# An attention and feed-forward kernel: its first loads, its idle products and its opening steps in another order

## The chip, the cores and the metric

The kernel runs on one core of one Trainium2 chip. The metric is the device time of one execution in microseconds (us); where several executions are shown, their median. Shorter is better.

The engines are named as in the profile: PE multiplies matrices, DVE (VectorE) and ACT (ScalarE) work on elements, POOL (GpSimd) does a little scalar work here, SP (SyncE) issues most of the transfers (DMAs). ACT issues a few of them at the start and at the end.

## The reference

Two parts follow each other. The first is an attention without softmax for 4 batches of 4 heads, 1088 positions and 32 columns each. A position's features are the 64 products of two sketches of 8 numbers, taken with the small matrices S1 and S2:

```python
def phi(x):
    a = np.einsum('rd,bhsd->bhsr', S1, x)
    b = np.einsum('rd,bhsd->bhsr', S2, x)
    return np.einsum('bhsi,bhsj->bhsij', a, b).reshape(*x.shape[:-1], r * r)
q_p, k_p = (phi(q), phi(k))
kv = np.einsum('bhsf,bhsd->bhfd', k_p, v)
z = np.sum(k_p, axis=2)
num = np.einsum('bhsf,bhfd->bhsd', q_p, kv)
den = np.einsum('bhsf,bhf->bhs', q_p, z)[..., None] + 1e-06
attn_out = num / den
```

The second part takes the 4352 resulting tokens of 128 columns through two matrix products with a rational function between them:

```python
h = x @ w_in                       # 128 -> 2048
P = a[0] + a[1] * h + a[2] * h**2 + a[3] * h**3
Q = 1.0 + np.abs(b[0]) * np.abs(h) + np.abs(b[1]) * h**2
out = (P / (Q + 1e-06)) @ w_out    # 2048 -> 128
```

## The kernel before

The whole program is one list of steps in an order written out by hand, `ORDER`, in the class `Fast`. (The class `General` is a second way through for coefficients that the first can't treat; it isn't entered here.) Each step is a name and a number, such as `kf1:0`. A loop goes through the list and emits each step's instructions on the engine that the step belongs to. Every engine then works through its own instructions strictly in that order; between engines only data and buffers are waited for. So a step's place in the list matters only against the other steps of the same engine. That holds for SP too, where the steps are transfers.

The opening, up to the first hidden layer, consists of these steps (the number behind the colon is a batch, a query block or a half):

- `load_v`, the two loads of S (into `s_raw`), those of the first batch's keys `k0`, of the first queries `q0`, and of `a` and `b` stand ahead of the list. The keys come in three transfers: the first four columns of each of four strips, the rest of three strips, and the rest of the last.
- `lx`, `lw`, `lk`, `lq`, `lv` load halves of `w_in`, halves of `w_out`, and keys, queries and v (`lq:0` is the rest of the first batch's queries). All are issued by SP.
- `tn` lets PE multiply a tile of zeros into a result that nobody reads, as often as `TURNS` says (`turn`, line 222).
- DVE turns S and spreads it (lines 250 and 255). Behind that, `kt0` to `kt3` turn the keys (line 315), `ks0` to `ks2` multiply them by S on PE (line 323), `kc` copies one sketch on ACT (line 330), `kf` multiplies the two sketches on DVE (line 335), and `kp0` to `kp2` multiply the features by v on PE (line 364). `kk` copies the sums (line 374).
- Query blocks go the same way: `qt` turns (DVE, line 387), `qs` sketches (PE, line 400), `qc` copies (ACT, lines 407 and 410), `qf` features (DVE, line 416), `qp` products with the keys' sums (PE, line 428), `qd`, `qi` and `qx` divide (lines 437, 444 and 449), `qb` turns back (PE, line 455), `qk` copies into `xT` (ACT, line 462). The blocks 0, 1 and 2 are the first three of the first batch; block 3 and all later ones send their sketches through memory and back (`Spread.copies`), on SP.
- `ba` takes the absolute values of b on ACT and starts a chain of small POOL instructions (`fitting`); `bi` is a reciprocal on DVE and more POOL work behind it (`factors`, line 775); `wo` scales halves of `w_out` by its results, on ACT or DVE (lines 711 and 713).
- `h2:0` is the first hidden layer (line 519), `e` its copy from PE's result buffer (line 525).

Behind the opening, a unit of tokens runs through the hidden layer, the rational function on DVE and ACT, and the second product (`G`, line 677), while the next batch's attention is interleaved. All of this is in `ORDER` too.

Of the kernel before, what the change touches and what calls it, by code (L numbers as in the profile page):

```python
# [28 lines left out]
pd0:0 u0:0 kc0:1 kc1:1 kf0:1 m0:0 kt0:2 ln1:0 h0:1 e2:1 kt1:2 ex1:0 e0:1 v0:0 rd1:0 h1:1 ks1:2 qs:4 kf1:1 h3:1 qt:5  # L29
e1:1 h1:2 v1:0 u0:1 qf:3 qc:4 ln0:0 kc1:2 e3:1 ex0:0 kp1:1 qp:3 pd1:1 kf1:2 h3:2 ln0:1 s1:0 e1:2 rd0:0 qd:3 qi:3 G3:0  # L30
h0:2 ex0:1 e3:2 kk:1 e0:2 G0:0 x1:0 G5:0 qx:3 u1:1 qf:4 qs:5 qp:4 s0:0 u0:2 ln1:1 h2:2 lq:2 lk:3 qc:5 qd:4 qi:4 ex1:1
qt:7 qx:4 qb:3 qk:3 qb:4 lv:2 qk:4 x0:0 rd0:1 m1:1 ks0:2 qs:7 e2:2 u1:2 ln0:2 rd1:1 h2:3 v0:1 h0:3 e2:3 h1:3 v1:1
kc0:2 kf0:2 kt1:3 s1:1 ex0:2 qt:9 qf:5 e0:3 e1:3 kt0:3 ln1:2 G3:1 G2:0 h3:3 x1:1 h0:4 qc:7 e3:3 h3:4 ra0:2 st:0 qp:5
ex1:2 qd:5 qi:5 e0:4 ra1:2 kp1:2 s0:2 qx:5 G0:2 qs:6 u1:3 pd1:2 e3:4 qb:5 h1:4 qk:5 m0:2 G0:1 m1:2 h0:5 s1:2 qf:7
ln0:3 qc:6 e1:4 ln1:3 h2:4 x0:2 v1:2 G2:1 e0:5 ex1:3 qt:8 x1:2 pd1:3 h3:5 G1:2 kk:2 e2:4 ks0:3 ex0:3 qp:7 u1:4 e3:5
qs:8 ln0:4 rd0:3 rd1:3 h2:5 qd:7 e2:5 G3:2 qf:6 qc:8 s1:3 h1:5 G2:2 kc0:3 ln1:4 G5:1 kf0:3 qi:7 e1:5 lq:3 ex0:4 ex1:4
h1:6 G5:2 m1:3 h3:6 qx:7 u1:5 G3:3 ra0:4 qs:9 qp:6 x1:3 G0:3 rd1:4 G2:3 e1:6 ln0:5 st:2 pd1:4 lv:3 s1:4 h0:6 e3:6
ln1:5 qd:6 qi:6 qb:7 qf:8 G4:3 qx:6 qk:7 h2:6 m1:4 e0:6 qc:9 G0:4 ex1:5 qb:6 qk:6 qp:8 qt:10 ks1:3 h2:7 e2:6 G3:4
ex0:5 u1:6 x1:4 e2:7 h0:7 qd:8 ln1:6 G5:3 rd1:5 qi:8 h3:7 G1:4 G5:4 qt:12 G1:3 e0:7 G2:4 pd1:5 rd0:5 ex1:6 e3:7 h1:7
m1:5 kc1:3 ra1:6 qf:9 ln0:6 qx:8 e1:7 qp:9 qs:10 ex0:6 v0:5 qd:9 h1:8 s1:5 G4:4 u1:7 pd1:6 qc:10 h3:8 e1:8 st:4 qt:11  # L40
v1:5 rd0:6 qi:9 qb:8 G3:5 ln0:7 kf1:3 e3:8 ln1:7 h0:8 h2:8 x1:5 qk:8 qs:11 e0:8 ex1:7 kp1:3 s1:6 qx:9 G0:5 e2:8 G5:5
ex0:7 h2:9 kk:3 qf:10 h3:9 u1:8 qb:9 ra0:7 m0:6 G0:6 ra1:7 qs:12 m1:6 qc:11 x0:6 ln0:8 v1:6 e3:9 pd1:7 e2:9 qp:10 qk:9
# [28 lines left out]
class General:  # L71
    FAST = False
    TURNS = (11, 0, 0, 0, 2, 0, 0, 0, 0)
# [49 lines left out]
def run(  # L123
# [70 lines left out]
    for i, s_in in enumerate((S1, S2)):  # L194
        t = consts.tile([128, D], FP, name=f"s_raw{i}")
        (nc.scalar, nc.sync)[i].dma_start(out=t, in_=bass.AP(tensor=s_in.tensor, offset=s_in.offset,
                                                             ap=[[0, 16], [D, R], [1, D]]))
        s_raw.append(t)
# [7 lines left out]
    nc.sync.dma_start(out=q0[:, 0:512], in_=q0_src[:, 0:512])  # L206
# [6 lines left out]
    nc.scalar.preload_act_table_set("abs_reciprocal_sqrt_and_small" if fast else "natural_log_exp_and_others")  # L213
    load_v(0)
# [59 lines left out]
    b_fit, c_fit, c_inv = (consts.tile([128, 2], FP, name=x) for x in ("b_fit", "c_fit", "c_inv"))  # L274
    a_k = consts.tile([128, 3], FP, name="a_k")
    special = consts.tile([128, 1], mybir.dt.int32, name="special")
    k_in_reg, k_sq_reg = (nc.scalar.alloc_register(x) if fast else None for x in ("k_in_reg", "k_sq_reg"))
    a1, a2, a3 = a_sb[:, 1:2], a_sb[:, 2:3], a_sb[:, 3:4]
# [370 lines left out]
    @skip()  # L649
    def d_v(i, h, hh):  # L650
        if horner(i, h):
            g = part_of(i, "g", h)
            nc.vector.tensor_scalar(out=g, in0=g, scalar1=a1, scalar2=None, op0=AX.add)

    @skip(plan.WIDE_X, horner)
    def d_g(i, h, hh):
        g = part_of(i, "g", h)
        nc.vector.tensor_mul(out=g, in0=g, in1=part_of(i, "s" if horner(i, first(h)) else "p", h))  # L658

    def terms(i):  # L660

        per = units[i][3]
        cuts = [(0, per // 2), (per // 2, per)]
        if i in plan.QUARTER:
            cuts[1:] = [(per // 2, 3 * per // 4), (3 * per // 4, per)]
        return [[(x, y, key) for x in range(*c)] if y != 1 or not horner(i, n) else []
                for n, c in enumerate(cuts) for y, key in enumerate(("r", "s", "g"))]
# [89 lines left out]
    def fitting():  # L757
        g = nc.gpsimd
        g.tensor_mul(out=sq, in0=ab0, in1=ab0)
# [5 lines left out]
        by(fit, b4, AX.is_ge, sq, AX.mult, fit)  # L765
        by(lim, fit, AX.mult, -1.0, AX.add, 1.0)
# [3 lines left out]
        g.tensor_copy(out=special, in_=lim)  # L770
        by(c_fit[:, 1:2], b4, AX.mult, 1.0 + 1e-6, AX.subtract, sq)
        g.tensor_copy(out=c_fit[:, 0:1], in_=b_fit[:, 0:1])

    def factors():
# [3 lines left out]
        nc.gpsimd.tensor_copy(out=a_k[:, 2:3], in_=k_out)  # L778
        by(k_in, b4, AX.mult, 0.5, AX.mult, c_inv[:, 0:1])
        by(k_sq, sq, AX.mult, c_inv[:, 1:2])  # L780

    def registers():
        nc.scalar.reg_load(k_in_reg, k_in[0:1, :].bitcast(mybir.dt.int32))
        nc.scalar.reg_load(k_sq_reg, k_sq[0:1, :].bitcast(mybir.dt.int32))
        if any(plan.P_ON_ACT):
            nc.scalar.reg_load(a3_reg, a_sb[0:1, 3:4].bitcast(mybir.dt.int32))
# [9 lines left out]
    does = {"e": evac, "h": hidden, "u": d_abs, "w": d_w, "y": d_y, "ln": a_square if fast else a_ln, "ex": a_root if fast else a_exp, "ra": a_inv, "rd": d_inv, "pa": a_p, "pd": d_p,  # L796
# [7 lines left out]
    for step in plan.ORDER:  # L804
# [63 lines left out]
```

## Time and profile before

| | |
|---|---|
| median of 3 runs | 251.57 us (251.22 to 251.88) |
| the profiled execution | 251.9 us |
| its span, first to last instruction | 250.0 us |
| PE busy | 240.5 us (96%) |
| DVE busy | 233.0 us (93%) |
| ACT busy | 227.9 us (91%) |
| POOL busy | 7.5 us (3%) |
| bytes moved | 19.60 MB, mean 78 GB/s |

Three engines are busy for over nine tenths of the span, so the busy time alone doesn't say which of them sets it. The profile's lines give a time from the span's start, a duration, the engine, the line of the code, the operation with its output and inputs, and in brackets how long the engine stood idle before it and what ended that. A number behind an x counts instructions; a matrix product in 32-bit floats appears as two of them.

### The profile page before, as it was taken

How to read it: one execution, taken by the hardware profiler on the slowest of the kernel's cores; microseconds unless marked ns; L12 is line 12 of the kernel's file. 1: busy time of each engine (PE TensorE's matmuls, PEld its weight loads, DVE VectorE, ACT ScalarE, POOL GpSimd, SP SyncE). 2: the span in 40 equal slices, each digit the busy share in tenths (PEclk: the TensorE clock that was granted, in tenths of full speed). 3: DMA queues.
4: the chain of work that ended last, by engine and by line, in shares of the span. 5: the costliest groups of instructions: out<-in, count | busy, mean ns of one | idle time of the engine just before them, and what ended most of it. 6: DMA issues, size and time to landing. Idle time of an engine off the chain costs nothing.

```text
span 250.0 us, 4083 instructions
## 1 busy us (share of the span) xinstructions
PE 240.5 (96%) x1585; PEld 133.8 (54%) x1585; DVE 233.0 (93%) x233; ACT 227.9 (91%) x217; POOL 7.5 (3%) x43
## 2 busy tenths in 40 slices
PE   7889999999999999999999999999999999999990
PEld 2668546645645455445555344444544467666770
DVE  3776999899999999999999999999999999999990
ACT  2267999999999999999999999999999999999980
POOL 4340000000000000000000000000000000000000
PEclk9999999999999999999999999999999999999999
DMA  5995348464413176210512200030020211020032
GB/s 155 257 387 89 99 121 188 134 156 78 144 27 100 28 202 138 69 45 16 148 22 77 67 3 0 16 102 3 0 42 0 40 25 22 0 37 8 0 49 42
DMA packets 30534, 19.60 MB, mean 78 GB/s; under 512 B 20400, under 2 KB 26672, under 8 KB 30512
## 3 DMA queue, kind: packets, MB, share of 16 engines
q1 hardware_dynamic: 28864, 18.92, 30.4%
q10 hardware_dynamic: 1648, 0.40, 0.9%
q8 instruction: 13, 0.21, 0.4%
q14 instruction: 9, 0.07, 0.1%
HBM read 16.16 MB, written 3.15 MB: 77 GB/s over the span
## 4 chain that ended last, share of the span: by engine, by line
PE 77%; DVE 13%; DMA 3%; issue 3%; SPq 0%; DVEq 0%
PE h_ps L519 42%; PE att_ps L677 23%; PE att_ps L428 4%; DVE g L658 4%; PE att_ps L364 4%; DVE g L647 3%; DVE s L643 2%; DMA k_sb<-in_k_dram 2%; PE att_ps L455 2%; DMA v_sb<-in_v_dram 2%; PE att_ps L473 2%; PE att_ps L323 1%; DVE p L600 1%; DVE r L630 1%; DVE out_sb L686 1%
## 5 line engine op out<-in xcount | busy, mean ns | idle before, releaser
L519 PE MATMUL h_ps<-xT,w_in_sb 128*128 128x512 f32 (+1 forms) x320 | 125.8, 532 | 0.0
L519 PEld LDWEIGHTS h_ps<-xT,w_in_sb 128*128 128x128 f32 x320 | 59.3, 190 | 44.4 <-issue 34.0
L525 ACT CAST hh<-h_ps 128x1024 bf16<-128x1024 f32 x68 | 72.2, 1086 | 2.1 <-PE h_ps L519 1.9
L613 ACT ACTIVATE ln<-u 128x2048 f32<-128x2048 bf16 (+1 forms) x35 | 67.2, 1950 | 0.0
L677 PEld LDWEIGHTS <-w_out 128*128 128x128 bf16 x432 | 41.8, 98 | 46.0 <-issue 16.5
L618 ACT ACTIVATE r<-ln 128x2048 bf16<-128x2048 f32 x22 | 44.0, 2002 | 0.0
L643 DVE TENSOR_TENSOR s<-hh,r 128x4096 bf16<-128x4096 bf16 (+2 forms) x21 | 39.2, 1872 | 0.0
L677 PE MATMUL att_ps<-r,w_out 128*128 128x512 bf16 (+1 forms) x160 | 34.8, 347 | 0.1
L677 PE MATMUL att_ps<-g,w_out 128*128 128x512 bf16 (+1 forms) x160 | 34.4, 347 | 0.0
L647 DVE TENSOR_TENSOR g<-hh,s 128x4096 bf16<-128x4096 bf16 (+2 forms) x16 | 27.8, 1744 | 0.3 <-PE att_ps L677 0.3
L658 DVE TENSOR_TENSOR g<-g,p 128x4096 bf16<-128x4096 bf16 (+2 forms) x15 | 27.7, 1849 | 0.0
L630 DVE TENSOR_TENSOR r<-r 128x2048 bf16<-128x2048 bf16 x22 | 26.5, 1217 | 0.0
L677 PE MATMUL att_ps<-s,w_out 128*128 128x512 bf16 (+1 forms) x112 | 24.5, 349 | 0.4 <-DVE s L643 0.4
L618 ACT ACTIVATE ln<-ln 128x2048 f32<-128x2048 f32 (+1 forms) x13 | 24.4, 1895 | 0.0
L624 ACT ACTIVATE r<-ln 128x2048 bf16<-128x2048 f32 (+1 forms) x13 | 23.7, 1868 | 0.0
L600 DVE TENSOR_SCALAR p<-hh,a_sb 128x4096 bf16<-128x4096 bf16 (+1 forms) x17 | 21.6, 1273 | 0.6 <-ACT hh L525 0.6
L548 DVE TENSOR_SCALAR u<-hh 128x2048 uint16<-128x2048 uint16 (+2 forms) x24 | 21.7, 905 | 0.4 <-ACT hh L525 0.4
L647 DVE TENSOR_TENSOR g<-hh,p 128x2048 bf16<-128x2048 bf16 (+1 forms) x7 | 11.6, 1663 | 0.0
L658 DVE TENSOR_TENSOR g<-g,s 128x2048 bf16<-128x2048 bf16 (+1 forms) x8 | 11.6, 1463 | 0.0
L428 PEld LDWEIGHTS att_ps<-kvz,q_pT 128*64 128x64 f32 x288 | 9.8, 137 | 3.3 <-issue 1.7
L428 PE MATMUL att_ps<-kvz,q_pT 128*64 128x66 f32 x288 | 11.1, 224 | 0.0
L364 PE MATMUL att_ps<-v_sb,k_p 128*64 128x64 f32 (+1 forms) x288 | 9.2, 222 | 1.0 <-DMA v_sb<-in_v_dram 1.0
(79 smaller groups left out, 146.6 us busy)
## 6 DMA issues: line engine op xcount, KB each, us to landing
a_all<-sk_d SPq DMA_DIRECT2D x6, 384.0 KB
b_all<-sk_d SPq DMA_DIRECT2D x12, 192.0 KB
v_sb<-in_v_dram SPq DMA_DIRECT2D x12, 144.0 KB
k_sb<-in_k_dram SPq DMA_DIRECT2D x3, 544.0 KB
q_sb<-in_q_dram SPq DMA_DIRECT2D x3, 544.0 KB
a_all<-sk_d SPq DMA_DIRECT2D x4, 320.0 KB
b_all<-sk_d SPq DMA_DIRECT2D x8, 160.0 KB
w_out_sb_f<-in_moe_w_out_dram SPq DMA_DIRECT2D x2, 512.0 KB
```

Of the source, the lines that this page charges most:

```text
L428: nc.tensor.matmul(self.nd[g * 64:(g + 1) * 64, o:o + 2 * KW], lhsT=self.q_p[:, c, x + g * 64:x + (g + 1) * 64], rhs=kvz[self.b % 2][:, c, ...
L519: nc.tensor.matmul(t[:, x * tl:(x + 1) * tl], lhsT=w_in_sb[:, f * 128:(f + 1) * 128], rhs=xT[:, x_at(t0):x_at(t0) + tl], start=True, stop= ...
L525: nc.scalar.copy(out=live[i]["hh"][:, part * PW:(part + 1) * PW], in_=live[i]["h", part])
L600: nc.vector.tensor_scalar(out=part_of(i, "p", h), in0=hh, scalar1=a3, scalar2=a2, op0=AX.mult, op1=AX.add)
L613: nc.scalar.activation(out=t, in_=live[i]["u"][:, span(h)], func=ACT.Square, scale=k_in_reg, bias=1.0)
L618: nc.scalar.activation(out=t if r_on_act(i, h) else part_of(i, "r", h), in_=t, func=ACT.Abs_reciprocal_sqrt, scale=k_sq_reg, bias=1.0)
L624: nc.scalar.activation(out=part_of(i, "r", h), in_=live[i]["ln", h], func=ACT.Square)
L630: nc.vector.tensor_mul(out=t, in0=t, in1=t)
L643: nc.vector.tensor_mul(out=part_of(i, "s", h), in0=hh, in1=part_of(i, "r", h))
L647: nc.vector.tensor_mul(out=part_of(i, "g", h), in0=hh, in1=part_of(i, "p" if horner(i, first(h)) else "s", h))
L658: nc.vector.tensor_mul(out=g, in0=g, in1=part_of(i, "s" if horner(i, first(h)) else "p", h))
L677: nc.tensor.matmul(outs[t0][:, :tl], lhsT=w_sb[y][:, f0 + x, :], rhs=part_of(i, key, h)[:, c:c + tl], start=done[0] == 0, stop=done[0] == ...
```

## The change

Three things are done. The transfers ahead of the list are given out differently: both loads of S are issued by SP, so that ACT's first issue is the first part of k; v comes ahead of the queries; b and a come last on ACT, behind the load of ACT's function table, b first. The idle products `tn:0` are eight instead of eleven, and the two of `tn:4` move from the head of the list to behind the key sketches. The first 132 of the 671 steps are put in another order; they are the same steps.

Besides, a second way to compute the numerator (`SQ`), and an addition done by a transfer (`VDMA`), are written into the code but switched off by empty tuples. What is left of them when they're off is a wider tile for the reciprocal and two more small copies on POOL, and the cast to `special` comes last in `fitting`.

```diff
-    TURNS = (11, 0, 0, 0, 2, 0, 0, 0, 0)
+    SQ = ()
+    VDMA = ()
+    WIDE_V = ()
+    TURNS = (8, 0, 0, 0, 2, 0, 0, 0, 0)
     ORDER = """
-tn:4 tn:0 lw:1 lq:0 kt0:0 lw:0 kt1:0 lx:1 kt2:0 lx:0 ks1:0 kt3:0 ks0:0 lk:1 qt:0 ks2:0 kc0:0 kc1:0 kf0:0 kf1:0 qs:0
-kc2:0 qt:1 kf2:0 qc:0 kp0:0 ba:0 kp1:0 qf:0 kp2:0 qt:3 qs:1 kk:0 bi:0 qt:2 lq:1 lv:1 qc:1 qf:1 qp:0 qd:0 qs:2 qi:0
-qx:0 qb:0 wo:3 qc:2 qk:0 qf:2 wo:0 qp:1 qs:3 qp:2 qd:1 wo:5 wo:1 h2:0 qd:2 wo:4 e2:0 qi:1 h3:0 qx:1 qi:2 h0:0 wo:2
-qx:2 qb:1 rg:0 kt0:1 e3:0 e0:0 qb:2 pd1:0 qk:2 h1:0 kt1:1 u1:0 m1:0 lk:2 qk:1 e1:0 qc:3 ks0:1 ks1:1 qt:6 qt:4 h2:1
...
+lx:0 kt1:0 tn:0 kt0:0 kt3:0 lq:0 kt2:0 ks0:0 ks1:0 ks2:0 tn:4 kc1:0 kf1:0 kc0:0 kf0:0 kc2:0 lx:1 kp0:0 qt:0 ba:0 kp1:0
+qs:0 kf2:0 qt:1 qc:0 qf:0 kp2:0 qt:2 kk:0 qs:1 qp:0 bi:0 qs:2 qc:1 lw:1 qd:0 qf:1 qi:0 qx:0 lk:1 qc:2 qb:0 qt:3 qk:0
+lw:0 qp:1 wo:5 qf:2 wo:1 lq:1 wo:3 qd:1 kt1:1 qs:3 kt0:1 lk:2 qc:3 qi:1 qp:2 h2:0 qd:2 e2:0 rg:0 qx:1 h3:0 qi:2 h0:0
+qx:2 wo:4 qb:2 wo:2 qb:1 ks0:1 e3:0 pd1:0 wo:0 ks1:1 e0:0 qk:1 u1:0 kc0:1 m1:0 qk:2 qt:4 h1:0 kt0:2 h2:1 ln1:0 e1:0
+h0:1 kf0:1 pd0:0 e2:1 kt1:2 m0:0 h1:1 ks1:2 kc1:1 qs:4 ex1:0 e0:1 u0:0 kf1:1 rd1:0 e1:1 kc1:2 qf:3 h3:1 lv:1 qc:4
...
-        (nc.scalar, nc.sync)[i].dma_start(out=t, in_=bass.AP(tensor=s_in.tensor, offset=s_in.offset,
+        nc.sync.dma_start(out=t, in_=bass.AP(tensor=s_in.tensor, offset=s_in.offset,
                                                              ap=[[0, 16], [D, R], [1, D]]))
...
     nc.scalar.dma_start(out=k0[:, km + 4 * D:S], in_=k0_src[:, km + 4 * D:S])
+    load_v(0)
     q0 = io.tile([128, S], FP, name="q_sb", bufs=1)
     q0_src = q[0].rearrange("h (g j) d -> (h g) (j d)", g=32)
     nc.sync.dma_start(out=q0[:, 0:512], in_=q0_src[:, 0:512])
+    nc.scalar.preload_act_table_set("abs_reciprocal_sqrt_and_small" if fast else "natural_log_exp_and_others")
     a_sb = consts.tile([128, 4], FP, name="a_sb")
     b_sb = consts.tile([128, 2], FP, name="b_sb")
+    nc.scalar.dma_start(out=b_sb, in_=bass.AP(tensor=moe_b.tensor, offset=moe_b.offset,
+                                              ap=[[0, 128]] + list(moe_b.ap)))
     nc.scalar.dma_start(out=a_sb, in_=bass.AP(tensor=moe_a.tensor, offset=moe_a.offset,
                                               ap=[[0, 128]] + list(moe_a.ap)))
-    nc.scalar.dma_start(out=b_sb, in_=bass.AP(tensor=moe_b.tensor, offset=moe_b.offset,
-                                              ap=[[0, 128]] + list(moe_b.ap)))
-    nc.scalar.preload_act_table_set("abs_reciprocal_sqrt_and_small" if fast else "natural_log_exp_and_others")
-    load_v(0)
...
-        g.tensor_copy(out=special, in_=lim)
+        if plan.SQ:
+            by(a_fit, a_sb[:, 2:4], AX.mult, fit, AX.add, lim)
+        else:
+            g.tensor_copy(out=a_fit, in_=b_fit)
         by(c_fit[:, 1:2], b4, AX.mult, 1.0 + 1e-6, AX.subtract, sq)
         g.tensor_copy(out=c_fit[:, 0:1], in_=b_fit[:, 0:1])
+        g.tensor_copy(out=c_fit[:, 2:4], in_=a_fit)
+        g.tensor_copy(out=special, in_=lim)
```

More of the change, by code (lines that the diff above doesn't have):

```diff
@@ L33 @@
[L33 to L42, printed above, removed]
@@ L72 @@
     FAST = False
+    SQ = ()
+    VDMA = ()
+    WIDE_V = ()
     TURNS = (11, 0, 0, 0, 2, 0, 0, 0, 0)
@@ L273, in run @@
     sq, lim, fit, b4, k_in, k_sq, k_out = (consts.tile([128, 1], FP, name=x) for x in ("sq", "lim", "fit", "b4", "k_in", "k_sq", "k_out"))
[L274 removed]
+    b_fit, a_lim, a_fit = (consts.tile([128, 2], FP, name=x) for x in ("b_fit", "a_lim", "a_fit"))
+    c_fit, c_inv, a_abs = (consts.tile([128, 4], FP, name=x) for x in ("c_fit", "c_inv", "a_abs"))
+    k_p, gam, delta = (consts.tile([128, 1], FP, name=x) for x in ("k_p", "gam", "delta"))
     a_k = consts.tile([128, 3], FP, name="a_k")
     special = consts.tile([128, 1], mybir.dt.int32, name="special")
[L277 to L278 removed]
+    k_in_reg, k_sq_reg, k_p_reg = (nc.scalar.alloc_register(x) if fast else None for x in ("k_in_reg", "k_sq_reg", "k_p_reg"))
+    a_n = consts.tile([128, 4], FP, name="a_n")
+    a_part = a_n if fast and plan.SQ else a_sb
+    a1, a2, a3 = (a_part[:, x:x + 1] for x in (1, 2, 3))
+    add_h, add_sq = a1, delta
+    kinds = [any(2 * i + h in plan.VDMA and 2 * i + h in x for i in range(17) for h in range(2)) if fast else False for x in (plan.HORNER, plan.SQ)]
+    RW = 1024 if all(kinds) else 2048
+    rows = [big.tile([128, RW], BF, name=f"row{x}") if kinds[x] else None for x in range(2)]
     a3_reg = nc.scalar.alloc_register("a3_reg" if fast else "a3_reg_g")
@@ L595, in first, with a_psq @@
         return 0 if h == "both" else h
+    @skip()
+    def a_psq(i, h, hh):
+        assert squared(i, h)
+        nc.scalar.activation(out=part_of(i, "g", h), in_=hh, func=ACT.Square, scale=k_p_reg, bias=1.0)
     @skip(plan.WIDE_P, on_act)
     def d_p(i, h, hh):
+        assert not squared(i, first(h))
         if not on_act(i, first(h)):
@@ L665, in terms @@
             cuts[1:] = [(per // 2, 3 * per // 4), (3 * per // 4, per)]
-        return [[(x, y, key) for x in range(*c)] if y != 1 or not horner(i, n) else []
+        return [[(x, y, key) for x in range(*c)] if y != 1 or not (horner(i, n) or squared(i, n)) else []
                 for n, c in enumerate(cuts) for y, key in enumerate(("r", "s", "g"))]
@@ L777, in factors @@
         by(a_k[:, 0:2], a_sb[:, 0:2], AX.mult, k_out)
-        nc.gpsimd.tensor_copy(out=a_k[:, 2:3], in_=k_out)
+        if not plan.SQ:
+            nc.gpsimd.tensor_copy(out=a_k[:, 2:3], in_=k_out)
         by(k_in, b4, AX.mult, 0.5, AX.mult, c_inv[:, 0:1])
         by(k_sq, sq, AX.mult, c_inv[:, 1:2])
-    def registers():
[L783 to L786, printed above, removed]
+        if plan.SQ:
+            by(gam, a_fit[:, 0:1], AX.mult, a_fit[:, 0:1])
+            by(gam, gam, AX.mult, 0.25, AX.mult, c_inv[:, 3:4])
+            by(a_k[:, 2:3], k_out, AX.mult, gam)
+            by(k_p, a_fit[:, 1:2], AX.mult, 2.0, AX.mult, c_inv[:, 2:3])
+            by(gam, k_p, AX.mult, 2.0, AX.mult, c_inv[:, 2:3])
+            by(a_n, a_sb, AX.mult, gam)
+            by(delta, a1, AX.add, -1.0)
+    def registers():
+        loads = [(k_in_reg, k_in), (k_sq_reg, k_sq)]
+        loads += [(k_p_reg, k_p)] * bool(plan.SQ) + [(a3_reg, a3)] * any(plan.P_ON_ACT)
+        for reg, x in loads:
+            nc.scalar.reg_load(reg, x[0:1, :].bitcast(mybir.dt.int32))
+        for row, x in zip(rows, (add_h, add_sq)):
+            if row is not None:
+                n = RW // 512
+                nc.scalar.activation(out=row.rearrange("p (c x) -> p c x", c=n), in_=idle[:, None, :].to_broadcast([128, n, 512]),
+                                     func=ACT.Identity, bias=x, scale=1.0)
     value = []
@@ L819, in run @@
             if fast:
+                if plan.SQ:
+                    nc.scalar.activation(out=a_abs, in_=a_sb, func=ACT.Abs)
                 fitting()
```

72 lines of the change are left out of this document (51 added, 21 removed).

## The prediction

> **What bounds the kernel now.** I read the busy time in wide stretches first, to see where any engine has time left.
>
> ```profile
> 0.00:18.00 18.00, 14.87 (x200) 9.32 (x200) 10.83 (x27) 5.68 (x16) 7.46 (x43) 1.00 0.87 262
> ...
> 46.00:201.00 155.00, 154.97 (x903) 76.62 (x903) 154.23 (x137) 154.60 (x141) 0.00 (x0) 1.00 0.26 64
> 201.00:240.00 39.00, 38.56 (x210) 26.25 (x209) 39.00 (x31) 39.00 (x30) 0.00 (x0) 1.00 0.13 20
> ```
>
> The columns are the stretch, its length, then PE, PE weight loads, DVE, ACT and POOL busy, the clock, the DMA share and GB/s. From 46 to 240 us PE, DVE and ACT are all busy to within a microsecond. The last 539 of the 671 steps stand in the same order as before, so that part costs the same and moves as a block. Time can be won only in the first 18 us, where PE is idle for 18.00 - 14.87 = 3.1 us. The second view is the chain that ended last, in order of time.
>
> ```profile
> 1.59 4.42 DMA k_sb<-in_k_dram
> ...
> 6.03 3.98 DMA v_sb<-in_v_dram
> ...
> 14.29 0.44 DVE qT L387
> ...
> 18.05 5.38 PE h_ps L519 x24
> 23.43 0.44 PE att_ps L455 x4
> ```
>
> The opening is: load k, load v, multiply keys by v (kp, line 364), query sketches (qs, 400), query products (qp, 428), with a wait for DVE's turning of the third query block (qT), turning back (qb, 455) and the first hidden layer (h2, 519). So I price the change by when h2 starts: 17.98 in PE's timeline.
>
> ```profile
> 1.26 5.69 PE L225 MATMUL att_ps<-idle 128*128 128x512 bf16 x13 [1.26 <-DVE idle L220]
> ...
> 8.08 1.13 PE L400 MATMUL h_ps<-qT,SAB 64*128 64x256 f32 x8
> 10.26 2.32 PE L364 MATMUL att_ps<-v_sb,k_p 128*64 128x64 f32 x72 [1.05 <-DMA v_sb<-in_v_dram]
> ...
> 13.57 0.69 PE L428 MATMUL att_ps<-kvz,q_pT 128*64 128x66 f32 x16
> 14.79 1.14 PE L400 MATMUL att_ps<-qT,SAB 64*128 64x256 f32 x8 [0.52 <-DVE qT L387]
> 16.22 0.41 PE L455 MATMUL att_ps<-ident,x_tok 128*128 128x128 f32 x2 [0.30 <-DVE x_tok L449]
> ...
> 17.98 1.35 PE L519 MATMUL h_ps<-xT,w_in_sb 128*128 128x256 f32 x5
> ```
>
> PE's holes are those in brackets: 1.05 us for v, 0.52 for qT, 0.30 for x_tok. Closing them all is worth 1.9 us, and that bounds the gain unless the key sketches also start earlier.
>
> **The loads.** Here are SP's and ACT's issues, SP's longest wait in that stretch, and what the DMA engines moved.
>
> ```profile
> 0.84 0.70 SPq L196 DMA_DIRECT2D s_raw<-in_S_dram  x1
> 1.59 0.81 SPq L201 DMA_DIRECT2D k_sb<-in_k_dram  x1
> 2.45 0.48 SPq L206 DMA_DIRECT2D q_sb<-in_q_dram  x1
> 2.98 3.36 SPq L187 DMA_DIRECT2D v_sb<-in_v_dram  x4
> ```
>
> ```profile
> 0.82 0.68 ACTq L196 DMA_DIRECT2D s_raw<-in_S_dram  x1
> 1.55 0.60 ACTq L199 DMA_DIRECT2D k_sb<-in_k_dram  x1
> ...
> 3.69 1.28 ACT L213 ACT_TABLE_LOAD   x1 [3.69 <-DMA s_raw<-in_S_dram]
> ```
>
> ```profile
> SPq L187 <- DMA k_sb<-in_k_dram: 1.8, 2, 1.3
> ```
>
> ```profile
> 0.00:8.40 8.40, 7.14 (x51) 3.22 (x53) 3.52 (x11) 1.61 (x3) 2.92 (x24) 1.00 0.69 169
> 8.00:9.50 1.50, 1.22 (x14) 0.70 (x10) 1.50 (x4) 0.53 (x2) 0.00 (x0) 1.00 0.68 138
> ```
>
> S (two times 16 KB), k (544 KB), the first queries (256 KB) and v (544 KB) are 1376 KB, or 1.41 MB. By 8.4 us 169 GB/s x 8.4 = 1.42 MB had moved, yet v landed only at 6.03 + 3.98 = 10.01, because two of its four parts were issued only after parts of k had landed (1.8 us of waits); the DMA share then fell to 0.68.
>
> Changed, ACT's first issue is k's first part, at 0.82 instead of 1.55. The second S moves behind the first on SP, from 0.82 to about 0.84 + 0.70 + 0.05 = 1.59, the rest of k from there to 2.3, v to 3.2, and the queries follow v. v's issues took 3.36 with 1.8 of waiting, so (3.36 - 1.8)/4 = 0.4 each without it, and the queries' issue is out near 5.3. Nothing of the 1.41 MB is then issued as late as 6.03. The bytes in front of v fall by 256 KB, those in front of the queries grow by 544 KB. The same bytes start at the same time, so the last of them, now the queries, land between 8.2 (no tail behind those 8.4 us and a little less waiting) and 9.6 (nearly v's 10.01). I take **L = 8.9**, the middle. v is one transfer of the queries ahead of them: 0.26 MB at the 262 GB/s of the first 18 us is 1.0 us, so v lands near 7.9.
>
> A rule speaks against the first part of the change. The Trainium skill, "DMA: Bandwidth & Descriptors", section "Issuing engines are not separate DMA queues", says that loads from different engines end on the same 16 DMA engines and interleave, so that a second issuing engine saves sequencer time alone. By it the swap of S and k is worth the 0.7 us of one issue at most. The sum here gives the swap nothing at all, for the reason that follows.
>
> **DVE before the sketches.**
>
> ```profile
> 3.00 0.51 DVE L250 STREAM_TRANSPOSE sT<-s_raw 128x32 f32<-128x32 f32 x2 [1.80 <-DMA s_raw<-in_S_dram]
> 3.44 0.30 DVE L255 TENSOR_TENSOR S<-sT,mask 128x32 f32<-128x32 f32 x2
> 5.24 1.63 DVE L315 STREAM_TRANSPOSE kT<-k_sb 128x256 f32<-128x256 f32 x4 [1.50 <-DMA k_sb<-in_k_dram]
> 7.19 0.45 DVE L387 STREAM_TRANSPOSE qT<-q_sb 128x256 f32<-128x256 f32 x1 [0.32 <-DMA q_sb<-in_q_dram]
> ...
> 9.42 1.45 DVE L335 TENSOR_TENSOR k_p<-h_ps,b_sk 128x1280 f32<-128x1280 f32 x1
> ...
> 14.21 0.17 DVE L775 RECIPROCAL c_inv<-c_fit 128x2 f32<-128x2 f32 x1 [1.05 <-POOL c_fit L772]
> ```
>
> All of k's turning (kt) stands behind S on DVE. S lands 2.2 us after its issue now (3.00 less 0.82), so the second at 3.8 if nothing is in its way, and by 5.2, when k's first part lands now, if k's 256 KB are. With 0.74 us of work on S, kt begins between 4.5 and 5.9, against 5.24; I take 5.3. It takes 1.63; the sketches start when the first pieces are turned, near 6.1 (the idle products are out of the way at 1.26 + 8 x 0.43 = 4.7) instead of 6.88. That lead of up to 0.8 us does not reach the end, since the queries are later.
>
> **The new path to the key products.** DVE's list is now kf1, kf0, qt0, kf2: kf2 stands behind the turning of the queries, so it ends at 8.9 + 0.05 + 0.45 + 1.45 = 10.85 (10.87 now). kp0 and kp1 are 32 of the 72 records of kp, at 2.32/72 = 0.032 each: 7.9 + 1.03 = 8.9. qs0 (1.13) runs from the turned queries at 9.4 to 10.6. The last 40 records take 1.29, with 0.05 of signal: kp ends at 10.85 + 0.05 + 1.29 = 12.2, against 12.58. **Gain 0.38**, and each microsecond of L is a microsecond here.
>
> **From the key products to h2.** Today qT of the third block stands behind the reciprocal of c_fit on DVE, which waited 1.05 us for POOL; changed, it stands ahead of it. With T for kp's end: qs1 to T + 1.1, qp0 (0.69) to T + 1.8, and qs2 directly behind, without the 0.52. Then these rows:
>
> ```profile
> 14.66 0.65 DVE L416 TENSOR_TENSOR q_pT<-h_ps,a_all 128x512 f32<-128x512 f32 x1
> 15.23 0.15 DVE L437 TENSOR_SCALAR den<-att_ps 128x8 f32<-128x8 f32 x1
> 15.41 0.20 DVE L444 RECIPROCAL rec<-den 128x8 f32<-128x8 f32 x1
> 15.65 0.42 DVE L449 TENSOR_TENSOR x_tok<-att_ps,rec 128x256 f32<-128x256 f32 x1
> ```
>
> den, rec and x_tok (0.77) now have qf1's 0.65 between them: with 0.2 of signals qb0 starts at T + 3.4, against 16.22 - 12.58 = 3.64. The 1.76 from qb0 to h2 stay. **Gain 0.24**, less than the 0.52, as x_tok is late next.
>
> **Costed at nothing.**
>
> ```profile
> 13.57 0.19 POOL L770 CAST special<-lim 128x1 int32<-128x1 f32 x1
> ...
> 13.99 0.18 POOL L772 COPY c_fit<-b_fit 128x1 f32<-128x1 f32 x1
> ```
>
> ```profile
> 15.18 2.30 SPq L187 DMA_DIRECT2D v_sb<-in_v_dram  x4
> 36.76 2.32 PE L364 MATMUL att_ps<-v_sb,k_p 128*64 128x64 f32 x72
> ```
>
> POOL gets two copies (0.18 each) ahead of the reciprocal and loses the cast (0.19): 0.2 later. b is now issued behind the table load (1.28). Its chain on POOL, done at 14.17 now, is needed at T + 1.9 = 14.1; half a microsecond more would use up the 0.24. The branches SQ and VDMA emit nothing. v of the next batch moves back on SP, behind the fourth query block's writes to its scratch and their reading back; from 15.18 to its reader at 36.76 there are over 20 us of cover. kT of the next batch moves ahead of the second block's reciprocal on DVE and so waits there for k; qb1, which needs that reciprocal, runs at 23.4, about 5 us behind. If k came later than that, PE would stop for the rest. In ACT's list one scaling of w_out moves behind the hidden layer's second copy, which only lets that copy go earlier.
>
> The sum: 0.38 + 0.24 = 0.62. The profiled execution lasted 251.9 us with a span of 250.0, so 1.9 lie around it; the median of the runs shown is 251.57. 251.57 - 0.62 = **250.9 us**.
>
> **The rivals.** *PE stays at half speed.* The thirteen idle products of 512 columns are 0.43 us apart; four of the same width from the chain, later:
>
> ```profile
> 69.64 0.86 PE att_ps L677 x4
> ```
>
> 0.215 each. So PE starts at half speed, and it was at full speed by kp, after 5.7 us of unbroken work. Changed, eight products end at 4.7, PE waits for kT until about 6.1, and two more follow the sketches. At half speed kp0, kp1 and qs0 take 2.06 and 2.26: 7.9 + 2.06 + 2.26 = 12.2, then kp2 ends at 13.5 at full speed or 14.8 at half. That is 0.9 to 2.2 behind 12.58; less 0.24, h2 is 0.7 to 2.0 later, and the middle is **252.9**. It decides if full speed comes after about 10.5, since kf2 leaves little slack. For it: the break. Against: from 6.1 on the work is nearly unbroken too. The Trainium skill, "TensorE: Matmul & The Clock Gate", Part 1, says that full speed comes after a busy window of about 3.4 us that runs freely. By it eight products, 3.4 us, fill a window only where it starts with them, and the work from 6.1 fills one by 12.9 at the latest, differently from run to run.
>
> *The queries land late.* If the order only moves the wait, L is 9.6 or later: kp ends at 12.9, and with the 0.24 h2 is where it was: **251.6**. For it: those bytes take until 8.4 today, and a landing lies behind its bytes. Against: today's v was held back by its issue.
>
> *The swap of S and k does nothing*: that is in the sum, which gives it no term.
>
> **How the numbers follow.** Forecast 0.66, half speed 0.18, late queries 0.16. A measurement of this kernel can tell about 0.3%, 0.75 us, from no change. The forecast is faster than that if L is below 8.8, or up to 9.1 if the later holes (0.52 + 0.30) close further: two thirds, 0.44, and 0.22 the same. Half speed: 0.15 slower, 0.03 same. Late queries: 0.13 same, 0.03 slower. Faster 0.44, same 0.38, slower 0.18. The range begins where all holes close (251.57 - 1.9 = 249.7) and reaches over the late queries into half speed: 249.7 to 252.5. The forecast alone is 249.7 to 251.6.
>
> **What would show it.** Line 364 no longer waits for v; DVE's first qT waits for q_sb until about 8.9; kp ends near 12.2; the 0.52 hole is gone; h2 starts near 17.4, with the chain behind it moved as far. It is wrong if h2 starts after 18, if lines 364 or 400 take twice their time, or if PE has a hole between 18 and 46.

## The result and the profile after

The changed kernel takes 254.15 us (median of 6 runs, 253.52 to 255.44) where the kernel before takes 251.80 on the same chip (6 runs, 251.22 to 252.09). The ratio is 1.0099, 95% interval 1.0073 to 1.0125: **slower by 1%, 2.35 us**, above the 252.5 at which the range ended. The profiled execution lasted 254.14 us with a span of 252.3 (before: 251.9 and 250.0).

The stretch between opening and end, shifted by two microseconds for comparison, in the columns of the first view of the prediction (changed kernel):

```profile
48.00:203.00 155.00, 153.91 (x890) 76.60 (x900) 153.31 (x136) 154.64 (x141) 0.00 (x0) 1.00 0.26 62
203.00:242.00 39.00, 38.41 (x208) 26.32 (x209) 39.00 (x32) 39.00 (x30) 0.00 (x0) 1.00 0.13 21
```

ACT is as full as before. From the start of the first hidden layer (h2) to the end of DVE's last instruction it is 226.61 us before and 226.56 after. So that part did move as a block, and the loss lies at the two ends. First the opening, TensorE's timeline of the changed kernel:

```profile
1.26 3.59 PE L231 MATMUL att_ps<-idle 128*128 128x512 bf16 x8 [1.26 <-DVE idle L226]
6.96 1.12 PE L337 MATMUL att_ps<-S,kT 128*64 128x64 f32 x16 [2.10 <-DVE kT L329]
...
10.04 1.98 PE L378 MATMUL att_ps<-v_sb,k_p 128*64 128x64 f32 x32
11.95 1.57 PE L414 MATMUL h_ps<-qT,SAB 64*128 64x256 f32 x8
13.45 1.39 PE L378 MATMUL att_ps<-v_sb,k_p 128*64 128x64 f32 x40
...
18.05 0.41 PE L469 MATMUL att_ps<-ident,x_tok 128*128 128x128 f32 x2 [0.46 <-DVE x_tok L463]
...
19.75 4.58 PE L533 MATMUL h_ps<-xT,w_in_sb 128*128 128x256 f32 x20
```

h2 starts at 19.75, not at 17.98, and not at the forecast 17.4. The 2.10 in brackets is a new hole behind the eight idle products. The 32 records of kp take 1.98 us, 62 ns each, where the 40 that follow take 35 ns each: the first part ran at half speed. The trace's record of the clock has TensorE at full speed from 12.88 us on, and from 6.79 in the kernel before.

What VectorE waited for, and SyncE's first issues and waits, in the same kernel:

```profile
5.79 0.21 DVE L256 STREAM_TRANSPOSE sT<-s_raw 128x32 f32<-128x32 f32 x1 [1.58 <-DMA s_raw<-in_S_dram]
...
6.14 1.59 DVE L329 STREAM_TRANSPOSE kT<-k_sb 128x256 f32<-128x256 f32 x4
...
9.98 0.45 DVE L401 STREAM_TRANSPOSE qT<-q_sb 128x256 f32<-128x256 f32 x1 [0.32 <-DMA q_sb<-in_q_dram]
10.35 1.45 DVE L349 TENSOR_TENSOR k_p<-h_ps,b_sk 128x1280 f32<-128x1280 f32 x1
```

```profile
0.84 1.32 SPq L202 DMA_DIRECT2D s_raw<-in_S_dram  x2
2.21 0.59 SPq L207 DMA_DIRECT2D k_sb<-in_k_dram  x1
2.84 3.25 SPq L193 DMA_DIRECT2D v_sb<-in_v_dram  x4
6.13 0.43 SPq L213 DMA_DIRECT2D q_sb<-in_q_dram  x1
```

```profile
SPq L193 <- DMA s_raw<-in_S_dram: 1.2, 1, 1.2
...
SPq L193 <- DMA k_sb<-in_k_dram: 0.5, 1, 0.5
```

The second half of S lands at 5.8 us instead of 3.0, everything of k on VectorE stands behind it, and v's issues wait 1.2 us for S and 0.5 us for k, where they waited 1.8 us for k alone. The queries are issued at 6.13 and land just before 9.98.

Then the end. The six last stores on SyncE and SyncE's longest waits there, before:

```profile
242.30 4.85 SPq L694 DMA_DIRECT2D out_dram<-out_sb  x6
```

```profile
SPq L836 <- SPq L836: 0.8, 2, 0.6
```

and after:

```profile
244.03 3.29 SPq L728 DMA_DIRECT2D out_dram<-out_sb  x6
```

```profile
SPq L900 <- SPq L900: 2.6, 1, 2.6
```

Lines 836 and 900 are the same line of the program: the branch behind which the engines skip the code of the second plan. SyncE went on 0.6 us after it before, and 2.6 us after it now; in exchange the issue of the stores was 1.6 us shorter. From the end of DVE's last instruction to the end of the span it is 5.38 us before and 6.03 after. The counts of the instruction queue, before and after, are the one other difference at this place:

```profile
q14 instruction: 9, 0.07, 0.1%
```

```profile
q14 instruction: 10, 0.08, 0.1%
```

One piece of 8 KB more of instructions was fetched. The change puts one DMA more on SyncE (S1, from ScalarE), and with it SyncE's branch is the 208th instruction of its list and no longer the 207th, counted in the two traces.

So in this execution 1.77 us were lost in the opening and 0.65 at the end. The experiments take the two apart.

### The profile page after: what moved, and what is told of

The parts are those of the page before. It is cut to its first block, busy times and chain, and to the rows that moved or that the text cites. A ratio compares the mean times of both kernels' runs of the same rounds, so it can differ in the third digit from the quotient of the medians.

```text
span 252.3 us, 4064 instructions
## 1 busy us (share of the span) xinstructions
PE 240.3 (95%) x1566; PEld 135.3 (54%) x1582; DVE 232.8 (92%) x233; ACT 228.0 (90%) x217; POOL 7.8 (3%) x45
## 4 chain that ended last, share of the span: by engine, by line
PE 33%; DVE 30%; ACT 19%; issue 7%; DMA 7%; SPq 2%; DVEq 0%; ACTq 0%
PE h_ps L533 15%; PE att_ps L711 12%; DVE g L692 7%; ACT ln L636 6%; ACT hh L539 5%; DVE g L670 5%; DVE s L666 4%; DVE r L653 3%; DMA b_all<-sk_d 3%; DVE p L623 2%; DVE u L562 2%; ACT r L641 2%; ACT ln L641 2%; ACT r L647 2%; DMA s_raw<-in_S_dram 2%
## 5 line engine op out<-in xcount | busy, mean ns | idle before, releaser
L711 PE MATMUL att_ps<-r,w_out 128*128 128x512 bf16 (+1 forms) x152 | 33.6, 346 | 0.7 <-issue 0.3
L711 PE MATMUL att_ps<-g,w_out 128*128 128x512 bf16 (+1 forms) x155 | 33.4, 346 | 0.3 <-issue 0.2
L378 PEld LDWEIGHTS att_ps<-v_sb,k_p 128*64 128x64 f32 (+1 forms) x288 | 9.7, 147 | 2.0 <-issue 1.1
```

Source lines behind the costliest of these rows:

```text
L711: nc.tensor.matmul(outs[t0][:, :tl], lhsT=w_sb[y][:, f0 + x, :], rhs=part_of(i, key, h)[:, c:c + tl], start=done[0] == 0, stop=done[0] == ...
```

## The experiments

Two theories compete, and turned out to add up. **Clock**: eight products and a late S leave TensorE at half speed through kp and qs. **Branch**: one instruction more on SyncE makes the end longer. The table has each run's median, what it is above the kernel before on the same chip ("less before"), and, of the profiled execution, the start of h2, the length of the end (from DVE's last instruction), SyncE's wait at the branch and the place of the branch in its list.

| run | edit | us | less before | h2 | end | wait | place |
|---|---|---|---|---|---|---|---|
| before | | 251.57 | | 17.98 | 5.38 | 0.6 | 207 |
| after | | 254.15 | +2.35 | 19.75 | 6.03 | 2.6 | 208 |
| e1 | after, 13 idle | 253.26 | +1.73 | 17.87 | 7.10 | 2.3 | 208 |
| e2 | after, S1 on ScalarE | 251.72 | +0.19 | 18.77 | 5.17 | 0.6 | 207 |
| e3 | after, queries ahead of v | 254.86 | +3.33 | 18.84 | 5.41 | 0.9 | 207 |
| e4 | before, 6 + 2 idle | 252.24 | +0.71 | 18.74 | 5.20 | 0.6 | 207 |
| e5 | before, one DMA more on SyncE | 252.80 | +1.16 | 17.68 | 6.88 | 2.1 | 208 |
| e6 | after, a store moved | 255.12 | +3.48 | 18.64 | 5.17 | 0.6 | 206 |
| e7 | e1, a store moved | 254.41 | +2.77 | 17.64 | 5.48 | 2.2 | 206 |
| e8 | after, 13 idle, S1 on ScalarE | 251.68 | +0.04 | 17.94 | 5.43 | 0.7 | 207 |
| e9 | after, a weight load on ScalarE | 252.24 | +0.46 | 18.38 | 5.22 | 0.6 | 206 |
| e10 | e9 with 13 idle | 251.53 | -0.25 | 19.05 | 5.16 | 0.6 | 206 |
| e11 | e8, queries and qs0 first | 251.22 | -0.56 | 17.78 | 5.30 | 2.0 | 206 |
| e12 | before, both loads of S on SyncE | 253.08 | +1.30 | 18.16 | 6.90 | 2.1 | 208 |
| f1, f2 | after, profiled twice more | 254.41, 255.28 | | 19.59, 19.92 | 6.55, 6.92 | 2.1, 2.2 | 208 |
| f3, f4 | e3, profiled twice more | 255.39, 254.23 | | 21.65, 19.54 | 5.34, 5.78 | 0.8, 0.9 | 207 |

**Thirteen idle products in the changed kernel (e1).**

```diff
-    TURNS = (8, 0, 0, 0, 2, 0, 0, 0, 0)
+    TURNS = (13, 0, 0, 0, 2, 0, 0, 0, 0)
```

> The changed kernel with thirteen idle products ahead instead of eight (tn:4's two stay where they are). Theory CLOCK: the five products bridge the 2.1 us in which PE stood idle before the key sketches, so PE reaches full speed near 7 us instead of 12.9; the two products behind the sketches (1.03), kp0 and kp1 (1.98) and qs0 (1.57) go back to about 0.5, 1.1 and 1.15, kp ends near 13.2 instead of 14.8, h2 starts near 18.1 instead of 19.75, and the time falls by 1.7 us to about 252.4. Rival LOADS (the second S and the queries land late, and that sets the opening): kp can't end before the queries' path, so at most 0.3 us are won, about 253.9.

Ratio 1.0056 (1.0028 to 1.0085). TensorE's timeline has kp and qs at full speed, though the second half of S is turned only at 5.22 us (both halves stood ready near 3.0 in the kernel before):

```profile
9.35 1.15 PE L378 MATMUL att_ps<-v_sb,k_p 128*64 128x64 f32 x32
10.44 1.13 PE L414 MATMUL h_ps<-qT,SAB 64*128 64x256 f32 x8
```

h2 starts at 17.87: the opening's loss is gone. A late S costs nothing while idle products keep the clock up: with S early (e8, below) h2 starts at 17.94. But only 0.6 of the 2.35 us came back, and the end was 7.1 us. That unexpected row led to the second theory.

**S1 back on ScalarE (e2).**

```diff
-        nc.sync.dma_start(out=t, in_=bass.AP(tensor=s_in.tensor, ...
+        (nc.scalar, nc.sync)[i].dma_start(out=t, in_=bass.AP(tensor=s_in.tensor, ...
```

> The changed kernel with the first S issued by ACT again, ahead of k, as before; all else as changed. LOADS: the second S lands near 3.3 instead of 5.8, kt starts near 5.3 instead of 6.14, and the time falls by 0.7 to 0.9 us. CLOCK: the key sketches start 0.7 us earlier, but PE is still at half speed until a window closes, between 9.5 and 12.9; kp, qs0 take as long as in the changed kernel, h2 starts 0.3 to 0.8 us earlier, so 253.3 to 253.8. The two agree on the sign; they differ in line 378's and line 414's durations (half speed or not).

Ratio 1.0005 (0.9987 to 1.0023): this edit alone takes back nearly all of the loss; what is left can't be told from nothing. The opening is still late, h2 at 18.77, since the clock is not at full speed throughout. The granted clock between 6.8 and 10.3 us is the column before the last two:

```profile
6.80:10.30 3.50, 2.75 (x37) 1.76 (x39) 2.36 (x6) 0.68 (x4) 1.01 (x5) 0.67 0.98 238
```

**The queries ahead of v (e3, and f3, f4).**

```diff
-    load_v(0)
     q0 = io.tile([128, S], FP, name="q_sb", bufs=1)
     ...
     nc.sync.dma_start(out=q0[:, 0:512], in_=q0_src[:, 0:512])
+    load_v(0)
```

> The changed kernel with the first queries ahead of v again. LOADS: the queries land near 7.5 instead of 9.96, and if their path over kf2 sets the end, h2 starts over 1 us earlier, 253.0; v then lands near 10. CLOCK: in the changed kernel PE is without a hole from 6.96 to 17.6, so nothing is won by earlier queries, and kp0 may wait for v: no change to 0.5 us slower, 254.1 to 254.7.

Ratio 1.0143 (1.0126 to 1.016). Its profiled execution was the quickest of its five, 252.59 us, and the others took over 2 us more, so the same kernel was profiled twice more:

> The changed kernel with the queries ahead of v, once more. If the opening is what varies: a longer execution (near 254.9 us) shows the first hidden layer at about 21 us with products at half speed for longer; if the end is: 5.4 us becomes 7 or more with the first hidden layer at 18.8; if neither: a stretch between 20 and 244 us that is 2.3 us longer than in the first profile (226.5 us from the first hidden layer to the last VectorE instruction).

> The same kernel a third time, with the same three readings: opening, end, or the stretch between.

It is the opening. TensorE in f3:

```profile
11.03 1.98 PE L378 MATMUL att_ps<-v_sb,k_p 128*64 128x64 f32 x32 [0.64 <-DMA v_sb<-in_v_dram]
12.93 2.08 PE L414 MATMUL h_ps<-qT,SAB 64*128 64x256 f32 x8
14.94 1.80 PE L378 MATMUL att_ps<-v_sb,k_p 128*64 128x64 f32 x40
...
21.65 0.70 PE L533 MATMUL h_ps<-xT,w_in_sb 128*128 128x256 f32 x2
```

With the queries first, v is late, and a hole stands ahead of kp: 0.64 us here, with full speed from 15.89 us, 0.47 in f4 with full speed from 10.74, 0.69 in e3 with full speed from 9.9. So the hole alone doesn't say when full speed comes. The same kernel's h2 starts anywhere from 18.84 to 21.65. This kernel has both loads of S on SyncE too, but one wait fewer in SyncE's list: the branch is at place 207 and the end is short, 5.3 to 5.8 us. So the load of S is not by itself what makes the end long.

**Eight idle products in the kernel before (e4).**

```diff
-    TURNS = (11, 0, 0, 0, 2, 0, 0, 0, 0)
+    TURNS = (6, 0, 0, 0, 2, 0, 0, 0, 0)
```

> The kernel before with six and two idle products at its head instead of eleven and two, and nothing else changed. CLOCK: the products end at 4.7, PE waits for kT until about 6.1, and half speed lasts to a window's end between 9.5 and 12.9: the time grows by 0.5 to 2 us, to 252.3 to 253.8. LOADS: nothing that sets the end is touched, 251.8 or slightly less as the sketches may start 0.7 us earlier.

Ratio 1.0027 (1.0013 to 1.0041). kp takes 2.90 us instead of 2.32 and h2 starts at 18.74, 0.76 later; the median is 0.71 higher. This is the price of the missing idle products by themselves.

```profile
8.13 1.86 PE L400 MATMUL h_ps<-qT,SAB 64*128 64x256 f32 x8 [0.22 <-DVE qT L387]
10.50 2.90 PE L364 MATMUL att_ps<-v_sb,k_p 128*64 128x64 f32 x72 [0.51 <-DMA v_sb<-in_v_dram]
```

**One DMA more on SyncE in the kernel before (e5).** It loads the factors a a second time; nobody reads them.

```diff
     nc.sync.dma_start(out=q0[:, 0:512], in_=q0_src[:, 0:512])
     ...
+    a_two = consts.tile([128, 4], FP, name="a_two")
+    nc.sync.dma_start(out=a_two, in_=bass.AP(tensor=moe_a.tensor, ...
```

> The kernel before with one instruction more on SyncE and nothing else: a second load of the four factors a into a tile that nobody reads, issued behind the queries. SyncE's comparison and branch at the end of the work is then its 208th instruction, as in the changed kernel, and not its 207th. Theory tail (the instruction behind SyncE's branch comes about 1.7 us later where the branch lies one place further): the opening is unchanged (first hidden layer at about 17.9 us), and the stretch from the last VectorE instruction to the end of the span grows from 5.4 to about 7 us: 253.3 us. Rival (the long tail of the run with thirteen idle products, 7.1 us, was its own, or comes from the loads of S): 251.5 us, tail 5.2 to 5.4.

Ratio 1.0035 (1.0019 to 1.005). The opening is none the worse (h2 at 17.68), and the end grows by 1.5 us. SyncE's rows, and the instruction queue:

```profile
242.13 4.63 SPq L697 DMA_DIRECT2D out_dram<-out_sb  x6
```

```profile
SPq L839 <- SPq L839: 2.1, 1, 2.1
```

```profile
q14 instruction: 10, 0.08, 0.1%
```

Here both stalls are there, the long issue of the stores (4.63) and the wait at the branch (2.1). A load of 2 KB in the first 8 us costs over a microsecond 240 us later.

**A store moved off SyncE (e6, and e7 with thirteen idle products).**

```diff
-                (nc.scalar if t0 + tl == n_tok and e % 2 else nc.sync).dma_start(
+                (nc.scalar if t0 + tl == n_tok and e % 2 or t0 == 0 and e == 3 else nc.sync).dma_start(
```

> The changed kernel with one early store of the output (the fourth of the first unit's) issued by ScalarE and not SyncE; SyncE's branch is then its 206th instruction. The opening is that of the changed kernel (first hidden layer near 19.75 us). Theory tail: the stretch behind the last VectorE instruction falls from 6.0 to about 5.3 us and the time to 252.7 to 253.4 us, with the rest of the loss left in the opening. Rival (all of the loss is the opening, and a long end is only the last stores' own): 254.1 us.

> The same move of one store in the changed kernel with thirteen idle products ahead. Theory clock and tail (two causes that add up): the first hidden layer at 17.9 us, the stretch behind the last VectorE instruction 5.2 to 5.4 us: 251.4 us, where thirteen idle products alone gave 253.3. Rival (the loss left at thirteen idle products is in the body): 253.3 us.

Both missed: 255.12 and 254.41, with an end of 5.17 and 5.48 as the theory had it, but with a body 2.5 us longer (229.1 from h2 to DVE's last end). My edit had a price of its own, seen in ScalarE's waits of e6: the store waits for VectorE's turning of the output, and ScalarE's queue stands still behind it.

```profile
ACT ln L641 <- DVE out_sb L720: 2.5, 1, 2.5
```

e7 also shows that the branch's place is not all: at place 206 it waited 2.2 us. There the last store's issue was short (0.43 us), as in the first profiled execution of the changed kernel (0.45).

**A load moved instead, for which ScalarE waits for nothing (e9, and e10 with thirteen idle products).** A wait of SyncE's goes with it, so the branch is two places earlier, at 206.

```diff
-        nc.sync.dma_start(out=w_in_sb[:, c], in_=moe_w_in[:, c])
+        (nc.scalar if plan.FAST and x else nc.sync).dma_start(out=w_in_sb[:, c], in_=moe_w_in[:, c])
```

> The changed kernel with the load of the second half of the first layer's weights issued by ScalarE and not SyncE; no store is touched, so ScalarE waits for nothing late. SyncE's branch then has the place that it has in the kernel before. Theory tail: the opening as in the changed kernel (first hidden layer at 18.8 to 19.8 us), the stretch behind the last VectorE instruction 5.2 to 5.4 us in place of 6.0 to 7.1: 252.6 to 253.5 us. Rival (the end is as long wherever the branch lies): 254.1 us.

> The same weight load moved in the changed kernel with thirteen idle products ahead. Theory clock and tail add up and nothing else is left of the loss: first hidden layer at 17.6 to 17.9 us, body as before, stretch behind the last VectorE instruction 5.2 to 5.4 us: 251.2 to 251.7 us, where thirteen idle products alone gave 253.3. Rival (a third loss, in the body): 252.5 us or more.

252.24 (ratio 1.0018, 0.9997 to 1.0039) and 251.53 (0.9993, 0.9979 to 1.0007). The branch of e9:

```profile
SPq L900 <- SPq L900: 1.2, 2, 0.6
```

With after and e1 these make a square. Less the kernel before on the same chip, the place of the branch is worth 1.89 us with eight idle products and 1.98 with thirteen; the idle products 0.62 at the later place and 0.71 at the earlier. In this square the two causes add up, and with both taken away nothing is left. A second square, of after, e1, e2 and e8 (below), has S1 back on ScalarE as its other edit: that is worth 2.16 us with eight idle products and 1.69 with thirteen, and the idle products 0.62 and only 0.15. So the idle products' share is not fixed to better than about 0.15 to 0.7 us. e10's profiled execution, 252.66, was the longest of its twelve (VectorE waited 2.45 us for its third block of queries, to 15.49 us); the other eleven took 251.32 to 252.50.

**S split and thirteen idle products (e8).** The edits of e1 and e2 together.

> The changed kernel with thirteen idle products and S1 back on ScalarE's queue, so that each half of S lands early and SyncE's branch keeps its place. Theory clock, S and tail: the sketches of k start near 6.1 us at full clock, the first hidden layer at 17.2 to 17.6 us, a short end: 250.6 to 251.1 us, below the kernel before. Rival (the queries' landing near 9.9 us sets what follows whatever the sketches do): the first hidden layer at 17.9 us and 251.4 us.

251.68, ratio 0.9996 (0.9984 to 1.0009), h2 at 17.94. The rival's h2 was right, but not its reason: the sketches start at 6.01, early as forecast, and then TensorE waits for v. For the products behind the queries it doesn't wait.

```profile
6.01 0.69 PE L337 MATMUL att_ps<-S,kT 128*64 128x64 f32 x16 [0.28 <-DVE kT L329]
...
9.49 1.15 PE L378 MATMUL att_ps<-v_sb,k_p 128*64 128x64 f32 x32 [0.65 <-DMA v_sb<-in_v_dram]
```

**Queries and their sketches first, on top of e8 (e11).**

```diff
-... lx:1 kp0:0 qt:0 ba:0 kp1:0 qs:0 kf2:0 ...
+... lx:1 qt:0 qs:0 kp0:0 ba:0 kp1:0 kf2:0 ...
```

and the queries' load ahead of v's, as in e3.

> The changed kernel with thirteen idle products, S1 back on ScalarE, the queries' load ahead of v's and the first block's transpose and sketches ahead of the first two products with v: what is left of the change is the order of the other opening steps and the loads of a and b. With v's landing near 10.4 us and 7.3 us of TensorE's work behind it, the first hidden layer comes at 17.7 us (17.94 with v first), the end short: 251.3 to 251.6 us, about the kernel before. Rival (the order of the other steps costs by itself): 252 us or more.

251.22 us, ratio 0.9978 (0.9963 to 0.9992): better than both kernels, though by less than the 0.3% that I said can be told. It is the changed kernel with S split, the queries ahead of v again and thirteen idle products; the order of the other opening steps is left. qs0 now fills part of the wait for v, and TensorE still waits 0.96 us for the queries:

```profile
9.49 1.14 PE L414 MATMUL h_ps<-qT,SAB 64*128 64x256 f32 x8 [0.96 <-DVE qT L401]
10.55 2.32 PE L378 MATMUL att_ps<-v_sb,k_p 128*64 128x64 f32 x72
```

**S alone (e12).** The kernel before with both loads of S on SyncE, the line of e2 the other way round.

> The kernel before with one part of the change alone: both loads of S on SyncE's queue. S is ready about 2 us later (near 5.9 us) but thirteen products (before's eleven and two) keep TensorE at work until 6.9 us, so the sketches start at about 6.9 us as before and the first hidden layer at 17.7 to 18.2 us. Theory tail: SyncE's branch is one place further, the stretch behind the last VectorE instruction 6.0 to 7.1 us: 252.7 to 253.2 us. Rival (only the opening counts): 251.6 us. Third case (the late S and the queries one step later on SyncE cost by themselves): first hidden layer after 18.5 us.

253.08, ratio 1.0055 (1.0035 to 1.0076). h2 starts at 18.16, 0.18 late, and the end is 6.90, 1.52 longer. This one line holds over half of the whole loss, nearly all of it at the end.

**The changed kernel again (f1, f2).**

> The changed kernel once more, as it is. If opening and end vary from execution to execution: first hidden layer at 18.4 to 18.7 us where the second half of S lands near 5.1 us, or 19.7 where it lands near 5.8; the stretch behind the last VectorE instruction 6.0 to 7.1 us; ten transfers of instructions on queue 14; 253.5 to 255.4 us. If the first profile is typical: 19.75 and 6.03 again.

> The same kernel a third time, with the same two readings: opening 18.4 to 19.8 us by the landing of S, end 6.0 to 7.1 us.

The opening is late each time (h2 at 19.59 and 19.92; S's second half turned at 5.17 and 5.72, full speed from 12.78 and 13.12), whichever way S lands: my expectation of 18.5 with an early S was wrong for f1. The end is 6.55 and 6.92.

## Why the prediction was wrong

- *"The last 539 of the 671 steps move as a block."* Right, within 0.05 us, and h2 was the right place to read the opening. Wrong was the silent assumption that the end behind it keeps its length. I costed the S load moved to SyncE by the landing of S alone and did not count the instruction that SyncE gains. Under "costed at nothing" it should have stood with a bound from both sides. It is the larger term by the medians (e5 +1.16, e12 +1.30, after to e9 1.89).
- *"PE stays at half speed"*, given 0.18, is what happened in all three profiled executions of the changed kernel. It was to decide if full speed came after 10.5 us: it came at 12.78 to 13.12. The sum of that rival, h2 0.7 to 2.0 later, holds the measured 1.77. My argument against it, nearly unbroken work from 6.1 us, failed at the break that I had named myself: the eight products end at 4.85, and the work begins 1.5 to 2.1 us behind them, at 6.34 to 6.96. Even with the work from 6.34 (f1) full speed came only at 12.78. With thirteen idle products (e1) it came at 5.17 and stayed. In e2 and e4 there is a full-speed stretch of 3.41 us behind the eight products, and it is lost again before kp. The Trainium skill's rule that I set beside it ("TensorE: Matmul & The Clock Gate", Part 1) gave 12.9 at the latest for work from 6.1. With the work's measured starts (6.96, 6.34, 6.89) the same estimate gives 13.8, 13.1 and 13.7, and the measured 12.88, 12.78 and 13.12 agree with it.
- *"The swap of S and k does nothing."* S's second half, due at 3.8 by my sum, landed just ahead of 5.79 (5.17 and 5.72 in f1 and f2), with k's first part issued before it. My bound for the start of kT, 4.5 to 5.9, was passed at 6.14. e1 beside e8 shows that this costs nothing where the clock stays up, so the term of zero was right on that condition only.
- *"0.4 each without it"* for v's issues was the step that mis-sized L. The 0.4 each was right, but the waits stayed, and I had put them at nothing: the issues took 3.25 us again, waiting 1.2 for S and 0.5 for k. So the queries went out at 6.13 and not 5.3, and L was near 9.96 (9.6 and 10.3 in f1 and f2), not 8.9, and beyond the 9.6 that I had as the late end. v, forecast for 7.9, landed at 9.2 to 9.5 where TensorE waited for it (e7, e8, e10). By my own formula (L + 3.3) kp then ends at 13.3 at full speed instead of 12.2. In e1, with L near 9.7, it ends at 12.97: 0.39 later than the 12.58 of the kernel before, not 0.38 earlier.
- *"Gain 0.24"* from kp's end to the turning back: 3.64 us before, 3.21 after (14.84 to 18.05), a gain of 0.43. The mechanism was right and the size nearly double. It is all that the new order brought.
- With both losses taken away (e10) the kernel is where it was, 251.53 beside 251.78, a difference within the noise: the forecast gain of 0.62 isn't there either. The opening of e1 says why: kp's end 0.39 later and the 0.43 behind it cancel.

Open stays how the loss divides exactly. Put into the kernel before one at a time, the missing idle products cost 0.71 us (e4) and one DMA more on SyncE 1.16 to 1.30 (e5, e12), together 1.9 to 2.0 of the 2.35. Three executions of the changed kernel put 1.6 to 1.9 us on the opening and 0.65 to 1.54 on the end; the square of medians puts 0.6 to 0.7 on the idle products and 1.9 to 2.0 on the branch's place. e9's profiled opening, with its full speed from 10.29, was a kind one, and moving a weight load may have helped the opening too; I didn't separate that.

Open is also the mechanism at the branch. Shown is that all six profiled executions at place 208 fetched a tenth piece of instructions within the span and waited 2.1 to 2.6 us, and that all twelve at 206 and 207 fetched nine (the page of e1 counts eleven, one of them of 88 bytes). In e7 and e11 the wait came with nine pieces as well, 2.2 and 2.0 us, but there the last store's issue was short and the whole end stayed at 5.3 to 5.5. It looks as if one stall of 1.5 to 2 us always falls near the end, in the one place or the other, and as if place 208 adds a second: five of its six executions have both, the first one of the changed kernel has the wait alone, of 2.6 us. The Trainium skill, "Runtime: NRT & Kernel Launch", section "Instruction fetch mechanics", says that a taken branch whose target is not among the pages at hand waits for a fetch by DMA. The times of the pieces on queue 14 agree with it in part: in all eight executions with a wait of 2.0 us or more, one or two pieces start between the branch and the moment when SyncE goes on (in the changed kernel at 248.34 and 248.63 us, with the branch done at 247.79 and SyncE going on at 250.40), and in the ten with 0.6 to 0.9 us none does. The tenth piece itself is not what SyncE waited for: it starts 0.6 to 0.8 us after SyncE went on (250.97 in the changed kernel). For which engine the pieces were fetched, and what was missing, no run here shows.

## What to carry to other kernels

Count the instructions that an edit adds to each engine, also to one that is idle, wherever code lies behind a branch that is taken at the end, and compare the instruction queue's count and the waits of the last two microseconds in both profiles. Idle products that hold the clock have to reach close to the first real work: thirteen that ended 1.11 us ahead of it kept full speed (e10), eight that ended 1.25 us or more ahead left half speed in part of the opening in every execution. Price a shortening by the hole that it leaves, and over several executions, not by the work behind the hole. When an experiment moves an instruction to prove a place in a list, move one that waits for nothing, or its own wait will drown the answer (e6 and e9).

## What was new of the hardware

- One DMA of 2 KB more in SyncE's list made the end of the kernel 1.5 us longer (e5), through a wait at a branch 240 us later.
- The clock changed in steps of 3.41 us whose place differs between executions: in e2 it was full from 4.57 to 7.98, half to 11.39, then full (e4, e6 and f4 have two such steps as well). In f3 full speed came at 15.89, in f4, the same kernel, at 10.74.
- A load of 16 KB landed 4.2 us after its issue when 256 KB of k had been issued ahead of it on the other engine and 48 KB were being issued, and 2.2 us after it when it went first (3.00 less 0.82 in the kernel before). In e3 and e7, with the same loads ahead, it took 3.8 and 3.5. This is its row in the chain of the changed kernel:

```profile
1.59 4.18 DMA s_raw<-in_S_dram
```
